# A fused adaLN block on one Trainium2 core: the last V product moved behind the first attention step, another place for the first score tile, and a later reciprocal

## The chip, the core and the metric

The kernel runs on one core of a Trainium2 chip. The core has five engines with queues of their own: PE (TensorE, the matrix products), ACT (ScalarE), DVE (VectorE), POOL (GpSimd) and SP (SyncE, which here issues nearly all DMAs). An engine works its queue strictly in order and waits on semaphores that the others raise. The metric is the device time of one execution in microseconds (us), lower is better. The kernel before takes 1149.5 us, the median of three runs (1148.99 to 1149.98).

## What is computed

One transformer block on x of 2048 tokens by D = 448, all in float32:

```python
x = A_x
mod = (_silu(c) @ w_mod).reshape(c.shape[0], 6, 1, -1)
sa, ca, ga, sb, cb, gb = ...
h = _layernorm(x) * (1 + ca) + sa
x = x + ga * _A_ref(h, A_wqkv, A_wo)          # 16 heads of 28, softmax over 2048 keys
h = _layernorm(x) * (1 + cb) + sb
x = x + gb * _B_ref(h, B_w1, B_b1, B_w2, B_b2)  # layernorm, 448 -> 1792, gelu, 1792 -> 448
```

Softmax is computed with the row maximum taken off, so every query row needs a maximum (or a value close to it) before its exponentials.

## The kernel before, in words

**Tiling.** Tokens come in four blocks of 512 (b, or qt as queries, cch as key chunks). The 16 heads of 28 are padded to 32 and taken in four groups g of four heads j. For precision each operand is split into a float32r part "hi" and a rest "lo", and a product is hi·hi + hi·lo + lo·hi.

**Phase 1** (the loop over `tasks`, line 595 on) makes Q, K and V. A task is (b, kind, g): kind 0 and 1 are Q and K of a head group (`qk_task`, products on line 339), kind 2 is V of 128 tokens (`v_task`, products on line 317, eleven matmuls of 448 columns, then an ACT copy on line 376). Q and K go to DRAM and are read back later. For block b = 3 there are ten tasks, n = 0 to 9: six of Q and K, then V(3,0) to V(3,3). Phase 1 has eight PSUM banks: two "pa" (the accumulators of the tasks, `ps_s`), five "mx" (`ps_mx`) and one "o" (`ps_o`).

**Maxima.** For a unit (g, qt) the maximum is taken over the four key chunks: for each 128 queries i, head j and chunk a one-matmul score (`max_mm`, line 392) goes to an mx tile and DVE reduces it (`max_one`, line 397). A unit has 64 of these. They stand in a list `mxq`, that of unit (0,0) first. `emit_task(n, sixth, n_pairs)` sends a few of them behind each task of phase 1, in place of idle time. Three units, (0,1), (0,2) and (0,3), take their first two chunks as pairs (list `pxq`, `pair_diff`): a product with the difference of the two key chunks, an ACT Relu (line 405), a product with the first chunk, and one DVE instruction that adds and takes the maximum (line 409), so that a pair costs two matmuls, one Relu and one DVE pass. `p1_n` holds what `emit_task` gets: the number of maxima, whether there is a sixth, and how many pairs.

**The shift of a unit.** When the last of a unit's 64 maxima is counted, `max_fin` (line 425) reduces them over the chunks, negated (DVE, line 429). `put`, two steps later (`tick_late`), transposes on DVE (line 436) and sends four small DMAs on SP (line 439), which write the maxima into row 28 of each head's 32 rows of the unit's Q tile (`qst`, tag `b0` or `b1`). The K tiles have ones in that row, so a score comes out with its maximum taken off. The score products of a unit read these rows. Behind the loop of phase 1 stand `finish_max(0, 0)`, which sends what is left of the maxima of unit (0,0), and `tick_late(True)`, which sends a waiting `put` at once (lines 678 and 679).

**Attention** is 16 units u = 4·g + qt of 16 steps (kt, 128 keys each). A step does: scores (line 1045, twelve matmuls in two halves, each into an "s" tile of two banks), three or four maxima of later units in between (`n_maxima`), two ACT exponentials (line 1050) into the tile `pt`, and then the product with V of the step before (`av`, line 1015, into the tile "o"). The tile `pt` rotates over the slots `ptags`. `c0` and `c1` also hold the normalised input of block 3, which V(3,·) reads; `d0` is also the scratch of the Relu of the pairs. In this phase "o" has a pool of its own, `share(3, 2)` gives three mx tiles and two s tiles.

**The end of a unit.** V has a column of ones, so "o" holds the sums of the exponentials too. `unit_end_tasks` lists (offset in steps, function): `t_den` fetches the sums with a DMA, `t_rec` inverts them on DVE (line 774), writes them to DRAM (line 776) and reads them back spread over the rows (line 778), `t_split` multiplies on POOL (line 783), `t_split2` makes hi and lo (DVE line 793, POOL line 794). Units whose output waits in DRAM until the last head group are "staged": units 0 to 10. The others go on to the output product (`t_wo`). The tasks of a unit's end run in steps 1 + offset of the next unit.

**MLP**: products with w1 (line 317 again) and w2 (lines 1102 to 1104), block after block.

Of the kernel before, what the change touches and what calls it, by code (L numbers as in the profile page):

```python
# [18 lines left out]
PSUM = bass.MemoryType.PSUM  # L19
# [9 lines left out]
NB = S // 512  # L29
# [12 lines left out]
def tile_adaln_block(ctx: ExitStack, tc: tile.TileContext, x, wqkv, wo, w1, b1, w2, b2, c, w_mod, out):  # L42
# [322 lines left out]

        return split

    def v_task(b, t):
        p = ps_s()
        ts = slice(t * 128, (t + 1) * 128)  # L370
        hh, hl = hT[b]
        mm_acc(p[:, :D], terms448(
            lambda k: hh(k)[:, ts], lambda k: hl(k)[:, ts], lambda k: wv[0][:, k, :], lambda k: wv[1][:, k, :],
        ))
        emit_task(*p1_n)
        act.copy(v_sb[b][:, t, :, :DH], p[:, :D].rearrange("p (h d) -> p h d", d=DH))


# [221 lines left out]
    for b in range(NB):  # L600
        more = b + 1 < NB
        tasks = []
        for g in range(1 if b else 0, NG):
            tasks += [(b, 0, g), (b, 1, g)]
        if b == 0:
            tasks[1], tasks[2] = tasks[2], tasks[1]
        tasks += [(b, 2, t) for t in range(4)]
        if more:
            stages, later = stages[-4:] if b else stages, ln1_stages(b + 2) if b + 2 < NB else None
            xs_next = []  # L610
            tasks[10:10] = [(b + 1, 0, 0), (b + 1, 1, 0)]
        for n, (tb, kind, g) in enumerate(tasks):
            post = []
            ready, newq = newq, []
            p1_n[0] = P1RATE if b < 1 else P1RATE + 1
            if not more and n == len(tasks) - 1:
                p1_n[0] = 0

            k = n - (5 if b < 2 else 4)
            p1_n[1] = not (more and (0 <= k < NC)) and not (b == 1 and n < 4)  # L620
            p1_n[2] = (3 if n > 4 else 1) if b == 3 else 2 if b == 2 and p1_n[1] else 1
            if kind < 2:
                fn = qk_task(tb, kind, g, 6, firsts[n]) if b == 0 and n < 2 else qk_task(tb, kind, g)
                if g == 0:
                    fn()
                else:
                    post.append(fn)
                if kind == 1 and (g == 0 or (g == 1 and tb < 2)):
                    newq = [(g, qt, cch) for qt in range(tb + 1) for cch in range(tb + 1) if max(qt, cch) == tb]
            else:  # L630
                v_task(tb, g)
            for item in ready:
                queue_max(*item)
            if b == 0 and 2 <= n < 6:
                prep_w(2, n - 2, act.copy, dve)
            if more:
                k = n - (5 if b < 2 else 4)
                if b == 0 and n < 4:
                    for fn in stages[2 * n : 2 * n + 2]:
                        fn(xs_next)  # L640
                if b and n < 4:
                    stages[n](xs_next)
                if 0 <= k < NC:
                    post.append(h_chunk(b + 1, xs_next, k))
                if later and 8 <= n < 12:
                    later[n - 8](None)
            if n == 6:
                v_init(b)
                if b == 0:
                    mod_load(0)  # L650
                    mod_load(1)
            if b == 2 and n == 5:
                sp.dma_start(b1_col, b1.rearrange("(k p) -> p k", p=128))
            if b == 1:
                if n < 2:
                    mod_mm(n)
                    mod_load(2 + n)
                elif n in (2, 3):
                    mod_mm(n)
                    if n == 3:  # L660
                        mod_fin()
            if not more:
                if n == 0:
                    load_q(0)
                    load_q(1)
                if n == 5:
                    load_k(0, 0)
                if n == 6:
                    act.activation(cols[:, 0:1], zero_col, AF.Exp)
                    for ch in range(1, 4):  # L670
                        load_k(0, ch)
            tick_late()
            for fn in post:
                fn()
        if more:
            stages = later
# [3 lines left out]
    ps1_cm.__exit__(None, None, None)  # L680


    o_pool[0] = ctx.enter_context(tc.tile_pool(name="po", bufs=1, space=PSUM))
    shared = []

    def share(n_mx, n_s):
# [3 lines left out]
        psp[:] = [shared[0].__enter__(), n_mx, n_s]  # L690

    share(3, 2)

    phase1[0] = False
    for item in deferred:
# [63 lines left out]
    def unit_end_tasks(u, o_sb):  # L759
        g, qt = divmod(u, NB)  # L760
        st = {}
        staged = g < last_g(qt)
        parts = [g] if g > last_g(qt) else list(range(g + 1))

        def t_den():
            q_ = pool if u == NU - 1 else sp
            den = sbt("den", [128, 16], bufs=2)
            q_.dma_start(den, o_sb[DH:128:32, :].rearrange("j (q r) -> j q r", r=16))
            st["den"] = den

        def t_rec():
            q_ = pool if u == NU - 1 else sp
            rec = st["den"]
            dve.reciprocal(rec, rec)
            drec = dr.tile([4, 512], F32, tag="drec", name=nm("drec"), bufs=2)
            q_.dma_start(drec.rearrange("j (q r) -> (j q) r", r=16), rec)
            rb = sbt("osb", [128, 512], bufs=2)
            q_.dma_start(rb, drec[:, None, :].broadcast_to([4, 32, 512]))
            st["rb"] = rb

        def t_split():
            st["on"] = st["rb"]
            pool.tensor_tensor(out=st["on"], in0=o_sb, in1=st["rb"], op=ALU.mult)  # L783

        def t_split2():
            on = st["on"]
            if u < NU - 1:
                hi = sbt("hi", [128, 512], F32R, bufs=3)
                lo = sbt("lo", [128, 512], F32R, bufs=3)
            else:  # L790
                hi = sb.tile([128, 512], F32R, tag=YTAGS[7], name="o_hi", bufs=1)
                lo = sbt("osb", [128, 512], F32R, bufs=2)
            dve.tensor_copy(hi, on)
            pool.tensor_tensor(out=lo, in0=on, in1=f(hi), op=ALU.subtract)
            st["hi"], st["lo"] = hi, lo
            if staged:
                for part in range(2):
                    sp.dma_start(f(doh[part][g])[:, qt * 512 : (qt + 1) * 512], f((hi, lo)[part]))

        def t_wo(t):  # L800
            def go():
                p = ps_mx()
                ts = slice(t * 128, (t + 1) * 128)
                terms = []
                for g_ in parts:
                    if g_ == g:
                        hi, lo = st["hi"][:, ts], st["lo"][:, ts]
                    else:
                        hi, lo = o_in[(qt, g_)][:, 0, ts], o_in[(qt, g_)][:, 1, ts]
                    w_hi, w_lo = wo_p[0][:, g_, :], wo_p[1][:, g_, :]  # L810
                    terms += [(hi, w_hi), (hi, w_lo), (lo, w_hi)]
                mm_acc(p[:, :D], terms)
                y = sbt("full", [128, 512], bufs=3)[:, :D]
                act.copy(y[:, :D], p[:, :D])  # L814
                pool.tensor_tensor(out=acc[qt][:, t, :], in0=acc[qt][:, t, :], in1=y[:, :D], op=ALU.add)

            return go

        tasks = [(0, t_den), (1, t_rec), (4, t_split), (5, t_split2)]
        if len(parts) > 1 and not staged:  # L820
            tasks.append((0, lambda: load_o(qt)))
        if not staged:
            tasks += [(7 + t, t_wo(t)) for t in range(4)]
        return tasks
# [192 lines left out]
                start=(kt == 0), stop=(kt == NKT - 1),  # L1017
            )

    ptags = ["c0", "c1", "d0"]  # L1020
    done_max = set()
    for u in range(NU):
        g, qt = divmod(u, NB)
        for kt in range(NKT):
# [15 lines left out]
            for hf in range(2):  # L1040
                s2 = ps_s2()
                for term, (kp, qp) in enumerate(((0, 0), (1, 0), (0, 1))):
                    for jj in range(2):
                        rows_ = slice(64 * hf + 32 * jj, 64 * hf + 32 * jj + 32)
                        pe.matmul(s2[:, jj, :], ks[rows_, kp, kc], qs[rows_, qp, :], start=(term == 0), stop=(term == 2))  # L1045
                    if hf == 0 and term < min(n0, n):
                        emit_max(1, 1)
                    if hf == 1 and ((term == 0 and n - n0 > 0) or (term == 2 and n - n0 > 1)):
                        emit_max(1, 0)
                act.activation(pt[:, 2 * hf : 2 * hf + 2, :], s2, AF.Exp, scale=SCALE)  # L1050
            if pend is not None:
                pu, pkt, pp, po = pend
                av(pu, pkt, pp, po)
# [99 lines left out]
```

## Time and profile before

| what | value |
|---|---|
| median of three runs | 1149.5 us |
| the profiled execution's own time | 1151.72 us |
| its span, first to last instruction | 1149.9 us |
| mean granted clock of TensorE | 0.997 |
| PE busy | 1137.5 us (99%) |
| DVE busy | 829.4 us (72%) |
| ACT busy | 682.6 us (59%) |
| POOL busy | 215.9 us (19%) |
| phase 1, first step of attention at | 180.61 us |

A line of the timeline has start, length, engine, line of the code, operation, output <- input, shape and count, and in brackets how long the engine sat idle before it and what ended that. A line of the waits has engine, tile and line <- what it waited for, then total us, number, longest. A line of the windows has the stretch, its length, busy us and count of PE, PEld (weight loads), DVE, ACT and POOL, then the granted clock of TensorE as a share, the DMA share and GB/s. Matmuls overlap, and a busy PE is not PE at its peak.

### The profile page before, as it was taken

The page shows a single profiled execution, that of the slowest core. Times are in us where ns is not written, and L with a number is a line of the kernel's source. Part 1 is how long each engine was busy: PE and PEld are TensorE (multiplying, and loading weights), DVE is VectorE, ACT ScalarE, POOL GpSimd, SP SyncE. Part 2 cuts the span into 40 slices and gives each one's busy share as a digit, 9 for nine tenths or more (in the row PEclk, how much of TensorE's full clock was granted, in tenths as well). Part 3 has the DMA queues.
Part 4 walks back from the last instruction along what each step waited for, and adds up shares of the span by engine and source line. Part 5 has one row for each costly group of instructions (what it writes and reads, how often), then busy time and mean ns, then how long its engine had stood idle before and what let it go on. Part 6 is the DMA issues. An engine that isn't in the chain of part 4 may idle for free.

```text
span 1149.9 us, 20811 instructions
## 1 busy us (share of the span) xinstructions
PE 1137.5 (99%) x8380; PEld 680.7 (59%) x8380; DVE 829.4 (72%) x1487; ACT 682.6 (59%) x839; POOL 215.9 (19%) x232
## 2 busy tenths in 40 slices
PE   8999999999999999999999999999999999999998
PEld 6767774444444444444444445545458888888887
DVE  6868787999888899989999876585448853444322
ACT  4666756777777887877777777675862321111110
POOL 2534431210000000000000011207214503223000
PEclk9999998999999999999999999999999999999999
DMA  9642354121132211321111221020323100000000
GB/s 301 205 147 111 101 184 129 38 66 57 35 98 73 57 38 38 91 65 56 53 57 30 84 84 53 33 84 2 118 62 95 43 33 1 1 32 1 32 1 32
DMA packets 51377, 81.08 MB, mean 71 GB/s; under 512 B 12728, under 2 KB 21772, under 8 KB 51280
## 3 DMA queue, kind: packets, MB, share of 16 engines
q1 hardware_dynamic: 50656, 79.01, 22.1%
q8 instruction: 66, 1.08, 0.4%
q10 hardware_dynamic: 288, 0.46, 0.1%
q0 software_dynamic: 336, 0.28, 0.1%
q14 instruction: 31, 0.25, 0.1%
HBM read 53.11 MB, written 26.35 MB: 69 GB/s over the span
## 4 chain that ended last, share of the span: by engine, by line
PE 95%; DMA 1%; DVE 1%; ACT 1%; issue 1%; SPq 0%; POOL 0%; DVEq 0%; POOLq 0%; ACTq 0%
PE s L1045 27%; PE o L1015 21%; PE mx L317 16%; PE pa L339 7%; PE mx L392 7%; PE s L1103 4%; PE s L1102 4%; PE s L1104 4%; PE pa L317 3%; PE o L240 1%; PE pa L276 1%; DMA drec<-den 1%; DMA osb<-drec 1%; ACT slot_c L1050 1%; PE mx L240 0%
## 5 line engine op out<-in xcount | busy, mean ns | idle before, releaser
L397 DVE TENSOR_REDUCE mxp<-mx 128x1 f32<-128x512 f32 x919 | 579.9, 684 | 106.5 <-PE mx L392 101.5
L1045 PE MATMUL s<-slot_b,slot_a 32*128 32x512 f32 x3072 | 385.5, 424 | 1.9 <-ACT full L814 0.7
L1050 ACT ACTIVATE slot_c<-s 128x1024 f32<-128x1024 f32 x342 | 331.6, 1022 | 86.3 <-PE s L1045 84.7
L1045 PEld LDWEIGHTS s<-slot_b,slot_a 32*128 32x128 f32 x3072 | 215.9, 184 | 255.2 <-ACT slot_c L1050 151.5
L392 PE MATMUL mx<-kh,qh 32*128 32x512 f32 x899 | 290.9, 471 | 1.4 <-DVE mxp L397 1.1
L1050 ACT ACTIVATE slot_d<-s 128x1024 f32<-128x1024 f32 x170 | 164.8, 1022 | 44.6 <-PE s L1045 44.5
L1015 PE MATMUL o<-slot_c,v 128*32 128x512 f32 x1368 | 184.4, 609 | 0.4 <-ACT osb L984 0.4
L1086 ACT ACTIVATE full<-mx,b_col 128x512 f32<-128x512 f32 x56 | 38.5, 688 | 191.9 <-PE mx L317 179.8
L1089 DVE CAST hi<-full 128x512 fp32r<-128x512 f32 x56 | 25.2, 450 | 135.3 <-ACT full L1086 135.3
L392 PEld LDWEIGHTS mx<-kh,qh 32*128 32x128 f32 x899 | 116.6, 182 | 9.6 <-DVE mxp L397 6.7
L783 POOL TENSOR_TENSOR osb<-osb,osb 128x512 f32<-128x512 f32 x16 | 20.9, 1307 | 484.3 <-DMA osb<-drec 412.3
L1015 PE MATMUL o<-slot_d,v 128*32 128x512 f32 x680 | 90.6, 605 | 0.0
L1015 PEld LDWEIGHTS o<-slot_c,v 128*32 128x32 f32 x1368 | 27.1, 108 | 57.5 <-issue 54.0
L317 PE MATMUL mx<-y,slot_a 128*128 128x512 f32 x160 | 60.6, 395 | 0.0
L405 ACT ACTIVATE slot_d<-mx 128x512 f32<-128x512 f32 x48 | 27.0, 596 | 40.1 <-PE mx L392 40.0
L1090 DVE TENSOR_TENSOR lo<-full,hi 128x512 fp32r<-128x512 f32 x56 | 44.1, 788 | 5.2
L317 PE MATMUL mx<-y,slot_c 128*128 128x512 f32 x152 | 47.5, 396 | 0.1
L1104 PE MATMUL s<-slot_v,lo 128*128 128x448 f32 x128 | 46.7, 365 | 0.0
L1102 PE MATMUL s<-slot_v,hi 128*128 128x448 f32 x128 | 46.6, 364 | 0.0
L317 PE MATMUL mx<-y,slot_v 128*128 128x512 f32 x112 | 39.2, 396 | 0.0
L317 PE MATMUL mx<-y,slot_b 128*128 128x512 f32 x112 | 39.0, 397 | 0.0
L339 PE MATMUL pa<-slot_c,slot_a 128*128 128x512 f32 x136 | 36.9, 405 | 0.0
(223 smaller groups left out, 1386.9 us busy)
## 6 DMA issues: line engine op xcount, KB each, us to landing
d<-lo SPq DMA_DIRECT2D x32, 256.0 KB
slot_b<-d SPq DMA_DIRECT2D x32, 256.0 KB
slot_a<-d SPq DMA_DIRECT2D x32, 256.0 KB
d<-hi SPq DMA_DIRECT2D x20, 256.0 KB
osb<-drec SPq DMA_DIRECT2D x15, 256.0 KB
out_dram<-xn SPq DMA_DIRECT2D x16, 224.0 KB
slot_v<-in_w_mod_dram SPq DMA_DIRECT2D x4, 784.0 KB
raw<-in_B_w_dram SPq DMA_DIRECT2D x14, 224.0 KB
```

What stands on the lines that cost most here:

```text
L317: pe.matmul(p, a, b, start=(i == 0), stop=(i == len(terms) - 1))
L339: pe.matmul(p, *ts[i], start=(i == 0), stop=(i == len(ts) - 1))
L392: pe.matmul(m, qh_sb[(g, qt)][js, i * 128 : (i + 1) * 128], k[js, :], start=True, stop=True)
L397: dve.tensor_reduce(out=mxp[(g, qt)][:, i, j, cch : cch + 1], in_=m, op=ALU.max, axis=AX.X)
L1015: pe.matmul(o[32 * j : 32 * j + 32, :], v_sb[kt // 4][:, kt % 4, 4 * g + j, :], p[:, j, :], start=(kt == 0), stop=(kt == NKT - 1),)
L1045: pe.matmul(s2[:, jj, :], ks[rows_, kp, kc], qs[rows_, qp, :], start=(term == 0), stop=(term == 2))
L1050: act.activation(pt[:, 2 * hf : 2 * hf + 2, :], s2, AF.Exp, scale=SCALE)
L1086: act.activation(gf, p, AF.Gelu_apprx_tanh, bias=b1_col[:, i : i + 1])
L1090: dve.tensor_tensor(out=glo, in0=gf, in1=f(ghi), op=ALU.subtract)
L1102: pe.matmul(pp, ghi[:, ts], w_hi, start=(m == 0), stop=False)
L1103: pe.matmul(pp, ghi[:, ts], w_lo, start=False, stop=False)
L1104: pe.matmul(pp, glo[:, ts], w_hi, start=False, stop=(m == NFT - 1))
```

## The change

Four edits.

- In phase 1 the tasks of block 3 are nine, not ten: V(3,3) is taken out of the list. Its products are issued in step 0 of attention, behind the step's scores and ahead of the product with V (there is none in step 0), into an mx tile, and three maxima are sent behind it.
- What phase 1 sends beside block 3's tasks: three pairs a task from n = 3 on and not from n = 5 on; in the last task (now n = 8, V(3,2)) two maxima, and its product goes to an mx tile and not to a pa tile.
- The pool of "o" is opened behind that of the s and mx tiles and on the other side of PSUM, so the first s tile lies on the two banks that were pa; `ptags` starts with `d0`.
- Staged units run `t_rec`, `t_split` and `t_split2` in offsets 4, 8 and 9, not 1, 4 and 5.

```diff
-    def v_task(b, t):
-        p = ps_s()
+    def v_task(b, t, p):
...
-        emit_task(*p1_n)
+        if phase1[0]:
+            emit_task(*p1_n)
         act.copy(v_sb[b][:, t, :, :DH], p[:, :D].rearrange("p (h d) -> p h d", d=DH))
...
-        tasks += [(b, 2, t) for t in range(4)]
+
+        tasks += [(b, 2, t) for t in range(4 if more else 3)]
...
             if not more and n == len(tasks) - 1:
-                p1_n[0] = 0
+                p1_n[0] = 2
 
             k = n - (5 if b < 2 else 4)
             p1_n[1] = not (more and (0 <= k < NC)) and not (b == 1 and n < 4)
-            p1_n[2] = (3 if n > 4 else 1) if b == 3 else 2 if b == 2 and p1_n[1] else 1
+            p1_n[2] = (3 if n > 2 else 1) if b == 3 else 2 if b == 2 and p1_n[1] else 1
...
-                v_task(tb, g)
+                v_task(tb, g, ps_mx() if p1_n[0] == 2 else ps_s())
...
-    o_pool[0] = ctx.enter_context(tc.tile_pool(name="po", bufs=1, space=PSUM))
     shared = []
...
     share(3, 2)
+    o_pool[0] = ctx.enter_context(tc.tile_pool(name="po", bufs=1, space=PSUM, side="right"))
...
-        tasks = [(0, t_den), (1, t_rec), (4, t_split), (5, t_split2)]
+
+        times = (0, 4, 8, 9) if staged else (0, 1, 4, 5)
+        tasks = list(zip(times, (t_den, t_rec, t_split, t_split2)))
...
-    ptags = ["c0", "c1", "d0"]
+    ptags = ["d0", "c0", "c1"]
...
                 act.activation(pt[:, 2 * hf : 2 * hf + 2, :], s2, AF.Exp, scale=SCALE)
+            if step == 0:
+                v_task(NB - 1, 3, ps_mx())
+                emit_max(3)
             if pend is not None:
```

## The prediction

> **What bounds the kernel now.** I read the page first (engines, chain), then the waits of PE and DVE, then the timeline of each engine where the change acts, then windows for the clock.
>
> ```profile
> PE 1137.5 (99%) x8380; PEld 680.7 (59%) x8380; DVE 829.4 (72%) x1487; ACT 682.6 (59%) x839; POOL 215.9 (19%) x232
> PE 95%; DMA 1%; DVE 1%; ACT 1%; issue 1%; SPq 0%; POOL 0%; DVEq 0%; POOLq 0%; ACTq 0%
> DVE den L774 <- DMA den<-osb: 8.6, 3, 4.4
> DVE hi L793 <- POOL osb L783: 2.9, 3, 1.7
> POOL osb L783 <- DMA osb<-drec: 412.3, 13, 37.4
> ```
>
> PE is the bound: 99% busy, 95% of the chain that ended last. A change pays only where it shortens PE's stream or a hole in it. Two places are touched. One is the seam between phase 1 and attention:
>
> ```profile
> 174.27 2.50 PE L317 MATMUL pa<-slot_e,slot_c 128*128 128x448 f32 x11
> 176.70 0.50 PE L392 MATMUL mx<-raw,qh 32*128 32x512 f32 x3
> 177.45 2.53 PE L317 MATMUL pa<-slot_e,slot_c 128*128 128x448 f32 x11
> 180.61 0.50 PE L1045 MATMUL s<-slot_b,slot_a 32*128 32x512 f32 x2 [0.62 <-ACT v L376]
> 182.74 0.50 PE L1045 MATMUL s<-slot_b,slot_a 32*128 32x512 f32 x2 [0.28 <-ACT slot_c L1050]
> 185.23 1.94 PE L1015 MATMUL o<-slot_c,v 128*32 128x512 f32 x8
> 189.43 1.51 PE L1015 MATMUL o<-slot_c,v 128*32 128x512 f32 x8
> 194.82 1.07 PE L1015 MATMUL o<-slot_c,v 128*32 128x512 f32 x8
> 180.00:183.00 3.00, 1.97 (x19) 1.15 (x21) 1.78 (x3) 1.87 (x3) 0.00 (x0) 1.00 1.05 393
> 183.50:184.00 0.50, 0.50 (x6) 0.35 (x5) 0.50 (x2) 0.33 (x2) 0.00 (x0) 0.55 0.93 185
> 186.00:189.00 3.00, 3.00 (x24) 1.47 (x16) 1.04 (x2) 0.58 (x2) 2.99 (x4) 0.50 0.15 41
> 190.00:190.50 0.50, 0.50 (x8) 0.00 (x0) 0.49 (x1) 0.50 (x1) 0.00 (x0) 0.62 0.30 86
> ```
>
> V(3,2) runs from 174.27, six products for maxima from 176.70, V(3,3) from 177.45; the first scores wait 0.62 us for its copy, step 1 waits 0.28 us for an exponential. In 180 to 183 PE is busy 1.97 of 3.00 us, and the granted clock then halves from about 183.55 to 190.4, some 6.8 us (0.55 and 0.62 are the slices in which it turns). So the first product with V comes 4.62 us after the first score, and the next three steps take 194.82 − 185.23 = 9.59 us. The other place is the reciprocal:
>
> ```profile
> 349.11 1.07 PE L1015 MATMUL o<-slot_d,v 128*32 128x512 f32 x8
> 351.33 1.06 PE L1015 MATMUL o<-slot_c,v 128*32 128x512 f32 x8
> 356.12 1.06 PE L1015 MATMUL o<-slot_c,v 128*32 128x512 f32 x8
> 351.15 0.58 SPq L768 DMA_DIRECT2D den<-osb  x1
> 353.05 0.26 DVE L774 RECIPROCAL den<-den 128x16 f32<-128x16 f32 x1 [2.63 <-DMA den<-osb]
> 346.37 1.06 PE L1015 MATMUL o<-slot_c,v 128*32 128x512 f32 x8
> 511.95 1.06 PE L1015 MATMUL o<-slot_c,v 128*32 128x512 f32 x8
> 515.68 1.06 PE L1015 MATMUL o<-slot_d,v 128*32 128x512 f32 x8
> 512.62 0.25 DVE L774 RECIPROCAL den<-den 128x16 f32<-128x16 f32 x1 [1.57 <-DMA den<-osb]
> ```
>
> Undisturbed steps take 2.74 and 2.22 us in turn (346.37, 349.11, 351.33). At 353.05 DVE stands still for the sums of unit 3; no maxima are reduced, PE finds no free mx tile, and the step takes 4.79 us. Unit 7 does the same at 512.62 with 3.73 us.
>
> **The change, part by part.**
>
> *The pairs come earlier, and that leaves maxima over.* This is the step that decides, and it stands in no line of the diff by itself. The 16 pairs of unit (0,3) are there from n = 1, and so are 16 singles of unit (0,0), its last key chunk, which head the list. A task with one pair sends four singles, a task with three sends none. Before: four singles in each of n = 1 to 4, so all 16 are out with n = 4. After: four in n = 1 and 2, none in n = 3 to 6, two in n = 7 (beside the last two pairs), two in n = 8. That is 12. The other four come from `finish_max(0, 0)`, behind V(3,2). In the built program's order six products of qh0 with kh3 stand between V(3,2) and the first score, where before there is only V(3,3). Only then is unit (0,0) complete; its reduction, transposition and four DMAs follow, and the first score reads what these write. Before, this was long past:
>
> ```profile
> 167.47 0.22 DVE L429 TENSOR_REDUCE m<-mxp 128x16 fp32r<-128x64 f32 x1
> 170.61 2.36 SPq L439 DMA_DIRECT2D slot_b<-full  x4
> 174.43 1.55 ACT L405 ACTIVATE slot_d<-mx 128x512 f32<-128x512 f32 x3
> 181.22 4.28 DVE L397 TENSOR_REDUCE mxp<-mx 128x1 f32<-128x512 f32 x7 [1.43 <-PE mx L392]
> 180.02 0.53 ACT L376 COPY v<-pa 128x448 f32<-128x448 f32 x1 [0.79 <-PE pa L317]
> 170.37 0.21 DVE L436 STREAM_TRANSPOSE full<-m 128x32 f32<-128x32 f32 x1
> ```
>
> Now the chain, with these durations, in before's time. V(3,2) started at 174.27 in pa; in mx it takes the tile of n = 7's first Relu, which is through at 174.43 + 0.52 + 0.1, so it runs 175.05 to 177.5 (its own 2.50 us). The six maxima follow. DVE starts its first reduction 0.61 us after the product (181.22 against 180.61): 178.1; six at 0.61 (4.28/7) end at 181.8. Reduction and transposition, 0.2 each: 182.2. SP issues four DMAs in 2.36 us, the last starting at 184.0; a small DMA lands 1.9 us after its issue starts (351.15 to 353.05): the first score at T = 185.9. PE has been idle since about 179.4, 6.5 us. Bounds of T: 185.3 (landing in 1.3 us) and 186.5.
>
> *V(3,3) behind step 0's scores.* The stretch from first score to first product with V was 4.62 us. V adds 2.53 us at full clock and 5.06 at half; it covers 0.41 us of holes (of the 1.03 us without PE in 180 to 183, less the 0.62). The third of the extra maxima takes V's mx tile and waits for its copy (0.53) and a reduction: 0.8 us, with 0 and 1.8 (three reductions in series) as ends. After a 6.5 us hole I expect half clock, as the smaller hole brought it. How long it lasts after T depends on a phase I don't know; I take 5 us, with the row's 6.8 as the long end, so V takes 3.8. First product with V: T + 4.62 + 3.8 − 0.41 + 0.8 = T + 8.8 = 194.7; ends T + 6.7 and T + 11.1. Three more steps at full clock are 7.4 us: 202.1 against 194.82, **+7.3 us** (185.3 + 6.7 + 7.4 gives +4.6; 186.5 + 11.1 + 7.4 gives +10.2).
>
> [...]
>
> *First s tile on the pa banks, d0 first.* The 0.62 us wait for V(3,3)'s copy goes, but the wait for the DMAs stands at the same place and covers it: nothing. `d0` is read last by the pairs' DVE pass, in n = 7: no wait. Step 1 writes `c0` only after V(3,3), which PE has done by then.
>
> *SP behind the moved DMAs.* The four now stand behind the K loads and ahead of three loads of maxima operands and of 16 wo loads.
>
> ```profile
> 177.59 1.39 SPq L420 DMA_DIRECT2D kh<-d  x2
> 179.98 12.46 SPq L726 DMA_DIRECT2D raw<-in_A_wo_dram  x16
> 200.94 0.38 DVE L733 CAST slot_e<-full 128x448 fp32r<-128x448 f32 x1
> ```
>
> These move back by some 7.6 us, but the DVE work on wo is in step 6 and moves back by 7.3 with the steps: nothing; without that cover, a DVE hole of up to 0.3.
>
> *Three maxima more in step 0.* The number in all stays, so three fewer come later, at the end of the list: −0.3 us (a step of four costs 2.74, one of three 2.22).
>
> *The later reciprocal.* It is asked for 3 steps (7.4 us) later, against holes of 2.63 and 1.57 us: both go. PE gains 4.79 − 2.74 and 3.73 − 2.74, 3.0 us. The 4.4 us hole in the wait's row is the last unit's, which isn't staged: it stays. Of the 2.9 us that DVE waits for POOL, 1.7 is one wait, I take it for the last unit's too; the other two, 0.6 each, cost PE between nothing (the holes above cost it 0.58 less than they are long) and 1.2: I take 0.4. Sum −3.4. Ends: −4.2 (all of 2.63 and 1.57) and −2.0, if the transfers, now between the K loads of steps 3 and 7, come late to step 9 and DVE waits anew. What is queued behind these waits is the maxima, and PE behind them.
>
> **Sum.** +7.3 − 0.3 − 3.4 = +3.6 us: span 1149.9 to 1153.5, the profiled execution 1151.72 to 1155.3. The median of the runs is 2.2 below that execution, so 1149.5 + 3.6 = **1153.1 us**.
>
> **Rivals.**
> - *The shift is in time (other side).* If the four DMAs landed by the time PE is through with the six maxima, 178.3, PE would have no hole, the clock would stay: first product with V at 178.3 + 6.7, three steps to 192.4, −2.4, with −3.4 and −0.3 that is −6.1: 1143.4. It speaks for it that before they had landed long ahead; against it that six reductions alone take 3.7 us behind the last product. It decides from T below 180.5. 0.09.
> - *The seam costs less.* The clock comes back at once and the extra maxima hide: at T + 6.7 it is +5.2, sum +1.5: 1151.0. For it: the phase is open. Against: 6.8 us in the row. 0.21.
> - *The reciprocal's gain isn't there.* New waits of the split and cast at steps 9 and 10 take the place of the old ones. For it: POOL waits for this transfer 13 times. Against: POOL has nothing else to do then, and DVE waited for it only 2.9 us in all. At zero gain and +7.3 − 0.3: 1156.5. 0.13.
>
> **How the numbers follow.** My own case has 0.57 and spans 1151.9 to 1155.2. A measurement tells 0.2%, 2.3 us, from no change: 1147.2 to 1151.8. Faster is the first rival, 0.09; the same is the second, 0.21; slower the rest, 0.70. For 8 in 10 I leave out the first rival and the outermost of the third: 1149.0 to 1156.5, which takes in the ends +0.1 (4.6 − 4.2 − 0.3) and, short of +7.9, most of the upper one.
>
> **What would show it.** Six reductions (line 397) behind V(3,2), then lines 429, 436 and four of 439 at about 182; a first score whose idle time of about 6.5 us ends on a DMA; half clock for 3 to 7 us behind it; V(3,3) between the scores of steps 0 and 1, in mx; no reciprocal of a staged unit with a wait ahead of it; steps of 2.74 at units 4 and 8. I am wrong if the first score starts below 182, if the clock stays full, or if new DVE waits show at line 793.

## The result, and the profile after

The changed kernel takes 1157.3 us (median of six runs, 1156.3 to 1159.2) against 1149.7 us for the kernel before on the same chip (six runs, 1148.6 to 1154.0): a ratio of 1.0057, interval 1.0042 to 1.0072, some 6.6 us slower. The profiled execution of the changed kernel took 1156.97 us, with a span of 1155.2 us and a mean granted clock of 0.995 (before: 1151.72, 1149.9, 0.997).

From the page of the changed kernel, busy time by engine and the chain by engine:

```profile
PE 1136.9 (98%) x8380; PEld 683.1 (59%) x8380; DVE 829.9 (72%) x1487; ACT 682.6 (59%) x839; POOL 215.9 (19%) x232
PE 95%; DVE 1%; ACT 1%; DMA 1%; issue 1%; SPq 0%; DVEq 0%; ACTq 0%
```

PE does the same work (1136.9 us, before 1137.5) in a span that is 5.3 us longer, so what was lost on balance is time in which PE stood idle. The waits of PE and DVE (engine, tile and line, what it waited for; us in total, number, longest) say which, and which went:

```profile
PE s L1048 <- DMA slot_b<-full: 6.6, 1, 6.6
PE mx L317 <- ACT slot_d L405: 0.7, 1, 0.7
DVE den L775 <- DMA den<-osb: 4.4, 1, 4.4
DVE hi L794 <- POOL osb L784: 2.4, 2, 1.7
```

One hole of 6.6 us is new: the first score waits for a DMA that writes its operand. Two of the three DVE waits for the sums of units are gone; the last unit's 4.4 us stays.

The seam in the timeline of the changed kernel, PE first, then what goes on meanwhile on DVE, SP's queue and ACT:

```profile
168.67 2.52 PE L317 MATMUL pa<-slot_e,slot_c 128*128 128x448 f32 x11
175.69 2.50 PE L317 MATMUL mx<-slot_e,slot_c 128*128 128x448 f32 x11 [0.72 <-ACT slot_d L405]
178.12 0.50 PE L392 MATMUL mx<-kh,qh 32*128 32x512 f32 x4
178.81 1.08 PE L392 MATMUL mx<-kh,qh 32*128 32x512 f32 x2 [0.19 <-ACT v L376]
186.53 0.79 PE L1048 MATMUL s<-slot_b,slot_a 32*128 32x512 f32 x2 [6.64 <-DMA slot_b<-full]
188.91 3.83 PE L317 MATMUL mx<-slot_e,slot_c 128*128 128x448 f32 x11
195.81 1.06 PE L1018 MATMUL o<-slot_d,v 128*32 128x512 f32 x8
198.54 1.06 PE L1018 MATMUL o<-slot_c,v 128*32 128x512 f32 x8
203.50 1.07 PE L1018 MATMUL o<-slot_d,v 128*32 128x512 f32 x8
...
178.65 3.68 DVE L397 TENSOR_REDUCE mxp<-mx 128x1 f32<-128x512 f32 x6 [1.31 <-PE mx L392]
182.37 0.22 DVE L429 TENSOR_REDUCE m<-mxp 128x16 fp32r<-128x64 f32 x1
182.68 0.21 DVE L436 STREAM_TRANSPOSE full<-m 128x32 f32<-128x32 f32 x1
182.92 2.33 SPq L439 DMA_DIRECT2D slot_b<-full  x4
```

The first row is V(3,0), from which I count below, since phase 1 ends up to some 2 us earlier or later from one profile to the next (V(3,0) starts at 168.03 to 170.22 us, and at 172.17 in the one kernel whose edit made phase 1 longer). V(3,2) and the six products of maxima are over at 179.9. Then DVE reduces six maxima, four of them the ones left over, closes the unit and transposes; SP issues four DMAs; the first score starts at 186.53. V(3,3) stands between the scores of steps 0 and 1 and takes 3.83 us instead of 2.53. From V(3,0) to the fourth product with V it is 203.50 − 168.67 = 34.83 us; before it was 194.82 − 168.03 = 26.79, with V(3,0) at

```profile
168.03 2.52 PE L317 MATMUL pa<-slot_e,slot_c 128*128 128x448 f32 x11
```

I call this stretch the seam: +8.04 us.

Windows of the same trace (stretch, its length, busy time and instructions of PE, PEld, DVE, ACT and POOL, the granted clock, the share and rate of the DMA engines):

```profile
181.00:181.50 0.50, 0.00 (x0) 0.00 (x0) 0.50 (x2) 0.00 (x0) 0.00 (x0) 1.00 0.04 16
181.50:182.00 0.50, 0.00 (x0) 0.00 (x0) 0.50 (x2) 0.00 (x0) 0.00 (x0) 0.61 0.00 0
186.00:191.50 5.50, 4.97 (x23) 3.90 (x24) 2.48 (x4) 1.94 (x2) 0.00 (x0) 0.50 0.71 207
191.50:192.00 0.50, 0.50 (x4) 0.44 (x3) 0.00 (x0) 0.00 (x0) 0.12 (x1) 0.65 0.12 36
```

The clock halves at about 181.6, 1.7 us after PE's last matmul, and comes back at about 191.85: 10.24 us in all, 5.3 us of it behind the first score. (The edges come from the slices in which the mean lies between 0.5 and 1: a mean of 0.61 over 0.5 us is 0.39 us at half clock.)

The places of the old reciprocal holes, from the third product with V of a unit to the fourth, in units 4 and 8:

```profile
359.84 1.06 PE L1018 MATMUL o<-slot_d,v 128*32 128x512 f32 x8
362.58 1.06 PE L1018 MATMUL o<-slot_c,v 128*32 128x512 f32 x8
...
518.40 1.06 PE L1018 MATMUL o<-slot_c,v 128*32 128x512 f32 x8
521.14 1.06 PE L1018 MATMUL o<-slot_c,v 128*32 128x512 f32 x8
```

The steps that took 4.79 and 3.73 us both take 2.74.

### The profile page after: what moved, and what is told of

It reads as the page before. It is cut to its first block, busy times and chain, and to the rows that moved or that the text cites. A ratio compares the mean times of both kernels' runs of the same rounds, so it can differ in the third digit from the quotient of the medians.

```text
span 1155.2 us, 20815 instructions
## 1 busy us (share of the span) xinstructions
PE 1136.9 (98%) x8380; PEld 683.1 (59%) x8380; DVE 829.9 (72%) x1487; ACT 682.6 (59%) x839; POOL 215.9 (19%) x232
## 4 chain that ended last, share of the span: by engine, by line
PE 95%; DVE 1%; ACT 1%; DMA 1%; issue 1%; SPq 0%; DVEq 0%; ACTq 0%
PE s L1048 28%; PE o L1018 22%; PE mx L317 16%; PE pa L339 7%; PE mx L392 6%; PE s L1109 4%; PE s L1110 4%; PE s L1108 4%; PE pa L317 3%; DMA slot_c<-in_w_mod_dram 1%; PE o L240 1%; PE mx L240 1%; DVE mxp L397 0%; PE o L547 0%; DMA acc<-in_A_x_dram 0%
## 5 line engine op out<-in xcount | busy, mean ns | idle before, releaser
L1018 PE MATMUL o<-slot_c,v 128*32 128x512 f32 x1360 | 181.2, 605 | 0.0
```

What stands on the lines that cost most here:

```text
L1018: pe.matmul(o[32 * j : 32 * j + 32, :], v_sb[kt // 4][:, kt % 4, 4 * g + j, :], p[:, j, :], start=(kt == 0), stop=(kt == NKT - 1),)
```

## The experiments

The theory at the start: the three pairs from n = 3 leave four maxima over, these put the first score behind a chain of reductions and DMAs, and the half clock that the hole brings makes the moved V product dear; the later reciprocal gives back a little over 3 us. The rival: moving the V product loses by itself. Each kernel is given with the edit against the one it starts from.

**The pairs as late as before, in the changed kernel** (e1_pairs_late).

```diff
-            p1_n[2] = (3 if n > 2 else 1) if b == 3 else 2 if b == 2 and p1_n[1] else 1
+            p1_n[2] = (3 if n > 4 else 1) if b == 3 else 2 if b == 2 and p1_n[1] else 1
```

> The kernel after, with three pairs a task from n = 5 on again (as before), so that no maxima of unit (0,0) are left over behind phase 1; all else stays changed. Theory (the shift of unit (0,0) is late): the DMA wait of the first score, 6.6 us, is gone; the first score waits only for the copy of V(3,2), which now stands behind three Relus, and starts about 180.3 to 181; V(3,3) and three maxima still lie between the scores, so the first product with V comes 7.4 to 9 us behind; with the later reciprocals 1146 to 1149 us, some 9 us under the kernel after. Rival (moving V(3,3) between the scores is itself what costs): 1155 us or more, whatever the wait.

1152.67 us, ratio 1.0013 (1.0004 to 1.0022, eleven runs): 5.1 us better than the change (0.0044 of 1150), yet not faster than before, as had been expected. Its timeline:

```profile
181.96 0.50 PE L1048 MATMUL s<-slot_b,slot_a 32*128 32x512 f32 x2 [1.56 <-DVE mxp L409]
184.03 4.48 PE L317 MATMUL mx<-slot_e,slot_c 128*128 128x448 f32 x11
192.61 1.94 PE L1018 MATMUL o<-slot_d,v 128*32 128x512 f32 x8
```

The wait for the DMAs is gone. In its place the first score waits 1.56 us for DVE's last pair pass, although that reads the o tile, on other banks than the first score's. It starts 12.67 us behind V(3,0) (169.29 in this trace); before it was 180.61 − 168.03 = 12.58, with V(3,3) already done by then. So taking V(3,3) from ahead of the first score did not bring the score forward, and V then costs its full length behind it, 4.48 us at half clock. The seam is 32.51 us, 5.7 longer than before. The time lies between the theory (1146 to 1149) and the rival (1155 or more): the theory missed, and the rival gains.

**The earlier pairs alone, in the kernel before** (e2_pairs_early_alone): the line above the other way round.

```diff
-            p1_n[2] = (3 if n > 4 else 1) if b == 3 else 2 if b == 2 and p1_n[1] else 1
+            p1_n[2] = (3 if n > 2 else 1) if b == 3 else 2 if b == 2 and p1_n[1] else 1
```

> The kernel before with one edit: three pairs a task from n = 3 on. V(3,3) stays in phase 1. One maximum of unit (0,0) is left over behind V(3,3). Theory: its reduction, line 429, 436 and the four DMAs hold the first score until about 185.5 (180.6 before), a wait of about 5 us for a DMA, half clock behind it: 1153.5 to 1155. Rival (the order of the maxima costs nothing): 1149.7 within 1.

1156.8 us, ratio 1.0051 (1.0037 to 1.0064): 5.9 us, somewhat over what was expected. Timeline:

```profile
186.31 0.79 PE L1045 MATMUL s<-slot_b,slot_a 32*128 32x512 f32 x2 [4.93 <-DMA slot_b<-full]
191.61 1.94 PE L1015 MATMUL o<-slot_c,v 128*32 128x512 f32 x8
```

V(3,3) now fills part of the hole, but the first score comes as late as in the change (186.31 − 169.10 = 17.21 us behind V(3,0); in the change 17.86). One number in one line costs 5 to 6 us in either kernel.

**The later reciprocal alone, in the kernel before** (e3_reciprocal_alone).

```diff
-        tasks = [(0, t_den), (1, t_rec), (4, t_split), (5, t_split2)]
+        times = (0, 4, 8, 9) if staged else (0, 1, 4, 5)
+        tasks = list(zip(times, (t_den, t_rec, t_split, t_split2)))
```

> The kernel before with one edit: staged units run the reciprocal, the split and the cast in offsets 4, 8 and 9. Theory: the long steps of units 4 and 8 (4.79 and 3.73 us) go back to 2.74, the wait of line 774 keeps only its 4.4 us of the last unit; 3.4 us gained, 1146.3 (1145.3 to 1147.7). Rival (new waits at the later place eat it): 1149.7 within 1, with waits of line 793 on POOL in several units.

1147.5 us, ratio 0.9972 (0.9961 to 0.9983): −3.2 us, as expected. It is faster than both kernels.

**The clock kept up in the hole of the changed kernel** (e6_keep_warm). 24 products with the identity, which nobody reads, ahead of the first score.

```diff
     tick_late(True)
+    busy = ps_s()
+    for _ in range(24):
+        pe.matmul(busy[:, :128], ident, ident, start=True, stop=True)
     ps1_cm.__exit__(None, None, None)
```

> The kernel after, with 24 matmuls of the identity (128 columns, as at the kernel's start, into a pa tile that nobody reads) behind the left-over maxima, to keep PE busy in the hole. Theory (hole and half clock add): the first score starts where it did, 186.5, but the clock stays at or near 1.0, V(3,3) takes 2.5 and not 3.8 us, the first product with V comes about 7.4 us behind the first score and not 9.3: about 2 us less than the kernel after, 1155.3. Rival (the half clock is hidden behind DVE and ACT): same as the kernel after, 1157.3 within 0.7.

```profile
186.12 0.50 PE L1051 MATMUL s<-slot_b,slot_a 32*128 32x512 f32 x2 [1.08 <-DMA slot_b<-full]
188.08 2.53 PE L317 MATMUL mx<-slot_e,slot_c 128*128 128x448 f32 x11
193.68 1.07 PE L1021 MATMUL o<-slot_d,v 128*32 128x512 f32 x8
```

The clock stays at 1.0, V takes 2.53 us, the first product with V comes 7.56 us behind the first score instead of 9.28, and the seam is 33.12 us, 1.7 shorter than in the change. The runs don't show a gain: 1157.71 us, ratio 1.0064 (1.0043 to 1.0085, four runs from 1155.9 to 1162.2). Three of the four ran at a mean granted clock of 0.999 or more and took 1155.9 to 1158.1 us, about what the change takes at 0.992 to 0.995 (1156.3 to 1159.2). So what the half clock costs the change isn't shown by the times; whether the 24 products cost as much as they save was not separated.

**V(3,3) back ahead of the first score, in the hole** (e7_v_in_the_hole). The first step's three extra maxima go too.

```diff
     tick_late(True)
+    p1_n[0] = 0
+    v_task(NB - 1, 3, ps_s())
     ps1_cm.__exit__(None, None, None)
...
-            if step == 0:
-                v_task(NB - 1, 3, ps_mx())
-                emit_max(3)
```

> The kernel after, with V(3,3) issued behind the left-over maxima and ahead of step 0 (into a pa tile), not between the scores of steps 0 and 1; the three extra maxima go too. Theory (the shift's DMAs set the first score): the first score starts where it did, about 17.9 us behind V(3,0), V(3,3) costs nothing in the hole, the first product with V comes 5.3 us behind the first score (9.3 in the kernel after): about 2.5 us less than the kernel after. Rival (V between the scores is hidden behind the exponentials): same as the kernel after within 0.7 us.

1154.52 us, ratio 1.0039 (1.0025 to 1.0053): 2.8 us less than the change by the medians, 2.1 by the ratios, with about 2.5 expected.

```profile
179.90 2.49 PE L317 MATMUL pa<-slot_e,slot_c 128*128 128x448 f32 x11
186.62 0.79 PE L1050 MATMUL s<-slot_b,slot_a 32*128 32x512 f32 x2 [4.22 <-DMA slot_b<-full]
191.91 1.94 PE L1020 MATMUL o<-slot_d,v 128*32 128x512 f32 x8
```

The first score starts where it did (17.88 us behind V(3,0)); the first product with V comes 5.29 us behind it instead of 9.28. So in the change V(3,3) and the three maxima behind it lie on the path, beside a hole in which V would have been free. Of these 3.99 us the three steps behind take back 1.45 (9.14 us against 7.69), since the half clock here lasts until 195.23, 8.6 us behind the first score. The seam is 2.5 us shorter.

**The moved V without the leftover, another way** (e8_v_move_no_leftover). In the changed kernel one maximum more per task for n = 1 to 4, and three pairs from n = 4.

```diff
-            p1_n[0] = P1RATE if b < 1 else P1RATE + 1
+            p1_n[0] = P1RATE if b < 1 else P1RATE + 2 if not more and 1 <= n <= 4 else P1RATE + 1
...
-            p1_n[2] = (3 if n > 2 else 1) if b == 3 else 2 if b == 2 and p1_n[1] else 1
+            p1_n[2] = (3 if n > 3 else 1) if b == 3 else 2 if b == 2 and p1_n[1] else 1
```

> The kernel after, with six maxima instead of five beside tasks n = 1 to 4 of block 3 and three pairs from n = 4 on: all 16 maxima of unit (0,0) are out with n = 4, and one pair instead of three stands beside the last task. Theory (moving V(3,3) loses by itself, because the first score still waits for all readers of phase 1's tiles, and V then lies on the path): the first score about 12.5 us behind V(3,0) as before the change, the first product with V 7.4 to 10 us behind it (4.6 before the change); against the kernel before +3 to +5 from the seam and -3.3 from the reciprocals: same to 0.2 per cent slower. Rival (only the left-over maxima and the late pairs cost): 4 to 5 us faster than the kernel before.

1154.95 us, ratio 1.0044 (1.003 to 1.0057), worse than expected.

```profile
183.57 0.50 PE L1048 MATMUL s<-slot_b,slot_a 32*128 32x512 f32 x2 [1.24 <-ACT v L376]
185.51 4.05 PE L317 MATMUL mx<-slot_e,slot_c 128*128 128x448 f32 x11
```

No DMA wait is left, but V(3,0) starts at 172.17 us, where the other profiles have 168.0 to 170.2: the added maxima made phase 1 itself some 2 to 4 us longer. So the time is no test of the seam; by the ratios of this run and the first experiment the four maxima cost some 3.6 us when moved ahead in this way, and 5.1 left over. The seam itself, counted from V(3,0), is 200.31 − 172.17 = 28.14 us, only 1.4 longer than before. With one pair instead of three beside the last task the first score comes 11.40 us behind V(3,0), and the half clock lasts 3.41 us. So what the moved V costs depends on the work beside V(3,2) and on the clock: the seam grows by 1.4 us here and by 5.7 in the first experiment.

**The places alone** (e11_banks_alone). In the kernel with the later reciprocal, the o pool on the right side, so that the first score tile lies on the pa banks, and V(3,3) in an mx tile, still ahead of the first score.

```diff
-        p = ps_s()
+        p = ps_mx() if (b, t) == (NB - 1, 3) else ps_s()
...
-    o_pool[0] = ctx.enter_context(tc.tile_pool(name="po", bufs=1, space=PSUM))
     shared = []
...
     share(3, 2)
+    o_pool[0] = ctx.enter_context(tc.tile_pool(name="po", bufs=1, space=PSUM, side="right"))
```

> The kernel before with the later reciprocals, the pool of o on the other side (first s tile on the two pa banks) and V(3,3) in an mx tile. Theory (the first tile of the new pool waits for all readers of the old pool): the first score still sits idle about 0.6 us for the ACT copy of V(3,3), though that tile lies in another bank. Rival (the wait is by bank): no wait, the first score follows V(3,3) at once.

One time, 1149.69 us, and one timeline:

```profile
178.81 2.49 PE L317 MATMUL mx<-slot_e,slot_c 128*128 128x448 f32 x11 [0.35 <-ACT slot_d L405]
181.93 0.50 PE L1046 MATMUL s<-slot_b,slot_a 32*128 32x512 f32 x2 [0.62 <-ACT v L376]
```

No phase 1 tile on the first score's banks is in use any more, and yet the score waits the same 0.62 us for the copy of V(3,3), which reads an mx tile. The pair pass on the o tile in the first experiment fits with this. In both cases (0.62 and 1.56 us) the first tile of the new pools waits for the last reader of a tile of the old pool that lies on other banks. (Which banks a tile has follows here from the order in which the kernel opens its pools; the trace names tiles, not banks.)

**The moved V alone** (e12_v_move_alone). The first experiment's kernel with the old reciprocal times, so neither leftover nor gain.

```diff
-        times = (0, 4, 8, 9) if staged else (0, 1, 4, 5)
+        times = (0, 1, 4, 5)
```

> The changed kernel with three pairs from n = 5 and the reciprocal's old times, so that no maxima are left over and the reciprocal's gain is out: only the moved V product, its mx tile, the swapped pools, the first maxima of step 0 and d0 first. Theory: moving the V product loses by itself, since the first score still waits for the last reader of phase 1's tiles and V then lies on the path at half clock: e1_pairs_late's +1.5 us with the reciprocal's 3.2 us taken back, +4.7 us, ratio 1.003 to 1.005; seam longer by 5 to 6 us. Rival: the reciprocal's gain is small beside the moved V product (its waits come at other places there), and the move costs little: ratio below 1.0025.

1154.96 us, ratio 1.0039 (1.0027 to 1.0051, twelve runs): 4.5 us, as the theory had it by now.

```profile
181.23 0.79 PE L1048 MATMUL s<-slot_b,slot_a 32*128 32x512 f32 x2 [1.56 <-DVE mxp L409]
183.59 4.40 PE L317 MATMUL mx<-slot_e,slot_c 128*128 128x448 f32 x11
191.07 1.86 PE L1018 MATMUL o<-slot_d,v 128*32 128x512 f32 x8
```

Again the first score comes 12.67 us behind V(3,0) (168.56), V takes 4.40 us, and the seam is 200.17 − 168.56 = 31.61 us, +4.8. One part of the rival's reason is seen all the same: with the old reciprocal times DVE waits only 0.27 us for the sums of unit 7 here, against 1.57 before, and the step takes 2.74 us; only unit 4's long step (4.36 us) is left.

**Later reciprocal, with and without filler** (e10_reciprocal_and_filler, then both once more beside each other). The filler is three products with the identity behind V(3,3) and four behind the scores of step 0, again read by nobody.

```diff
     tick_late(True)
+    busy = ps_s()
+    for _ in range(3):
+        pe.matmul(busy[:, :128], ident, ident, start=True, stop=True)
...
+            if step == 0:
+                idle = ps_mx()
+                for _ in range(4):
+                    pe.matmul(idle[:, :128], ident, ident, start=True, stop=True)
```

> The kernel before with the later reciprocals and filler: three matmuls of the identity behind V(3,3), four behind step 0's scores, which nobody reads. Theory (half clock in the seam of the kernel before costs some 2 to 3 us): the clock stays at 1.0, the three steps behind the first product with V take 7.5 us and not 9.6: 2 us less than the later reciprocals alone, 4.5 to 5.5 us faster than before. Rival (DVE and ACT set the pace there, as where filler was tried in the kernel after without a clear gain): the same as the later reciprocals alone, 3.2 us faster.

> e3_reciprocal_alone once more, beside the kernel with filler products on the same chip. Theory: ratio 0.996 to 0.9985 against the kernel before.

> e10_reciprocal_and_filler once more (seven products with the identity that nobody reads, beside the later reciprocal). Theory A: the clock kept full in the seam is worth what the profile showed, 1 to 2 us: a ratio 0.001 to 0.0015 below that of e13_reciprocal_again. Theory B: the runs show none of it (the filler delays what it stands ahead of, or the clock falls elsewhere): the two ratios within 0.0005 of each other, or the filler's higher.

With filler: 1148.67 us, ratio 0.9981 (0.9971 to 0.9992), then 1148.72 us, 0.9975 (0.9963 to 0.9988). Without: 1147.16 us, 0.9971 (0.9957 to 0.9985). The filler is not seen to gain anything, as theory B has it. It costs time itself: of the last two kernels, on one chip, the runs at a mean granted clock of 0.999 or more have a median of 1148.3 us with filler (9 of 12) and 1146.9 without (7 of 10). The seam accounts for 0.5 us of this (194.92 − 170.22 = 24.70 us in the last profile with filler; 24.20 without, below); where the rest lies was not found. And the filler did not keep the clock up everywhere: that profile has it at half from about 23.5 to 27 us (means of 0.97 from 0 to 25 us and of 0.96 from 25 to 50), far ahead of the seam. Why there is little to gain shows in two profiles of the same kernel, the later reciprocal alone. First execution, 1149.38 us:

```profile
180.00:184.00 4.00, 2.95 (x25) 1.72 (x25) 2.60 (x7) 2.13 (x4) 0.00 (x0) 1.00 1.05 397
184.00:188.00 4.00, 4.00 (x23) 1.38 (x23) 2.61 (x5) 2.77 (x3) 0.52 (x1) 0.57 0.51 142
```

Second execution, 1146.93 us:

```profile
180.00:184.00 4.00, 3.00 (x23) 1.73 (x21) 2.57 (x7) 2.10 (x5) 0.00 (x0) 1.00 1.05 402
184.00:188.00 4.00, 3.95 (x38) 1.85 (x38) 3.37 (x6) 2.99 (x4) 0.96 (x1) 1.00 0.61 163
```

The same holes (2.95 and 3.00 of 4 us busy), and the clock halves in one execution and not in the other. The seam is 195.91 − 169.19 = 26.72 us in the first and 193.55 − 169.35 = 24.20 in the second: 2.5 us, as much as the two times lie apart (2.45). So these small holes go with the half clock in some executions only (5 of the 17 runs of this kernel have a mean granted clock below 0.999), and there is little left for a filler to save.

**The kernel before, profiled again** (e15_before_again), no edit.

> The kernel before, unchanged, profiled once more. The same kernel with the later reciprocal showed the seam at half clock in one profiled execution (1149.38 us) and at full clock in another (1146.93 us), 2.45 us apart. Theory: the profiled execution of before (1151.72 us, 2.2 us above the median of its runs) is one with the half clock, and most of its runs have none: this one then shows full clock in 183 to 192 us, steps of 2.74, 2.16 and 2.80 us behind the first product with V, and a time of 1148.5 to 1150 us. Rival: the kernel before halves its clock there in nearly every execution, and the 2.2 us come from elsewhere: half clock again at 183 to 192 us, whatever the time.

```profile
181.03 0.49 PE L1045 MATMUL s<-slot_b,slot_a 32*128 32x512 f32 x2 [0.62 <-ACT v L376]
186.00:188.00 2.00, 2.00 (x12) 0.48 (x8) 0.00 (x0) 0.78 (x1) 1.09 (x2) 0.50 0.19 54
```

1151.25 us, and again at half clock; the run beside it took 1149.38 us at a mean granted clock of 1.0, against 0.997. The rival's picture came out for this execution, but not its reason: of the 59 runs of before beside the other experiments, 32 ran at 0.999 or more. Both profiled executions of before have the half clock, and both lie about 2 us above what most runs take.

## Why the prediction was right, and where it was wrong

The direction held (0.70 on slower). The forecast was +3.6 us, and 6.6 came. On the 1149.5 us that the forecast started from, the ratio gives 1156.1 us (1154.3 to 1157.8), just inside the range that ended at 1156.5 and above the 1155.2 of its own case; the median itself, 1157.3, lies 0.8 us above the range. In 1150 us the parts that the runs separate are, in order, before → moved V alone → with the later reciprocal → with the earlier pairs: ratios 1, 1.0039, 1.0013, 1.0057, that is **+4.5, −3.0, +5.1 us**, together +6.6. Each part has an interval of some 1.4 to 2 us to either side, the runs were made on different chips (each against before on its own), and another order would divide the sum otherwise.

- *The pairs leave maxima over, and the chain starts the first score late.* Right in mechanism and size. T, the first score, was forecast at 185.9 in before's time; it is 186.53 in a trace that runs 0.64 us later by then, so 185.89. Six reductions, lines 429 and 436, four DMAs at 182.92 and a hole of 6.64 us (6.5 forecast) are all there. The last of the DMAs starts at 184.73, 1.80 us ahead of the score (1.9); the landing in 1.3 us of T's lower bound was an estimate that no run shows. Two experiments, with and without the leftover, price it at 5.9 and 5.1 us.
- *V(3,3) behind step 0's scores.* V takes 3.83 us (3.8; the 5.06 us for a V wholly at half clock were twice 2.53, and late pairs, where it ran so, took 4.48), the half clock lasts 5.3 us behind T (5), the first product with V comes 9.28 us behind T (8.8). The three steps behind it take 203.50 − 195.81 = 7.69 us (7.4), since the steps run at 2.73, 2.16 and 2.80. With 0.5 and 0.3 us more, the seam is +8.04 instead of +7.3: the term that was mis-sized, by 0.7 us, inside its own ends.
- *The 0.62 us wait for V(3,3)'s copy goes.* Wrong in its reason. In two cases, the places alone (0.62 us) and the late pairs (1.56 us), the first score waited for a reader of a phase 1 tile on other banks than its own. Here the DMA wait covers it, so the price of nothing stands. But the same error makes the first rival, "the shift is in time", wrong by its own condition: with the DMAs landed in time, it had the first product with V at 178.3 + 6.7 and 1143.4 us; the kernel with the late pairs has its DMAs landed in time and takes 1152.67 us, because the first score still waits until 181.96 and V then runs at half clock (in its profile, the slowest of its runs). The forecast counted 5.3 us for the late T and 4.2 for V behind it, less 2.2 for steps at full clock; it did not see that V's place loses by itself, 4.5 us by the runs, also where T is not late.
- *The later reciprocal, −3.4.* Right for the kernel before: −3.2 us alone, −3.3 when repeated. In the profiles, from the fourth product with V to the first of unit 12, before takes 666.85 − 194.82 = 472.0 us, the later reciprocal alone 468.7, the change 672.12 − 203.50 = 468.6. Part of the gain by the ratios may be the clock: runs at 0.999 or more, compared on the same chip, give −2.2 and −2.5 us. With the V product moved the same stretch takes 670.94 − 200.17 = 470.8 us, and with the later reciprocal beside it 670.58 − 201.80 = 468.8: 2.0 us there, since unit 8's hole was gone already, and not the 3.0 of the ratios. In the change both steps went to 2.74 us, the last unit's 4.4 us stayed, DVE's waits for POOL fell by 0.5 only, and no new wait came. The rival without the gain is out.
- *Three maxima more in step 0, −0.3; the moved DMAs of SP, nothing.* Neither was separated. The sum of the terms leaves 8.04 + 0.64 − 5.25 = 3.4 us of gain behind the seam in the profiles, for the reciprocal's −3.4 and this −0.3 together.
- *From the profiled execution to the median.* This step failed most. The sum gave 1155.3 us for the profiled execution; it took 1156.97, of which 0.64 us had passed by the start of V(3,0) and 0.7 is the seam. Then I took off 2.2 us, since before's profiled execution lay that far above its median. The change's profiled execution lies at its median (1156.97 against 1157.3). The table holds the hole ahead of the first score against this difference:

| kernel | hole, us | half clock in the profile, us | profiled | median | runs at 0.999 or more |
|---|---|---|---|---|---|
| before | 0.62 | 6.8 | 1151.72 | 1149.7 | 32 of 59 |
| later reciprocal alone | 0.62 | 6.8 | 1149.38 | 1147.5 | 5 of 7 |
| the same, again | 0.62 | none | 1146.93 | 1147.2 | 7 of 10 |
| V moved, more maxima per task | 1.24 | 3.41 | 1153.94 | 1155.0 | none of 5 |
| moved V alone | 1.56 | 10.24 | 1155.46 | 1155.0 | none of 12 |
| late pairs in the change | 1.56 | 13.65 | 1156.17 | 1152.7 | 2 of 11 |
| V in the hole | 4.22 | 10.24 | 1154.41 | 1154.5 | none of 4 |
| earlier pairs alone | 4.93 | 10.24 | 1156.43 | 1156.8 | none of 4 |
| the change | 6.64 | 10.24 | 1156.97 | 1157.3 | none of 6 |

The last column counts runs by the mean granted clock of the whole execution, which is on record for each (for before, the runs beside the experiments). A stretch of 6.83 us at half clock takes this mean to 0.997, one of 10.24 us to 0.995 or 0.996 (the profiles in the table). The 32 runs of before at 0.999 or more took 1148.2 to 1150.9 us (median 1149.5), the other 27, at 0.994 to 0.998, took 1150.2 to 1155.4 (median 1152.1), and its profiled execution is one of the latter. All six runs of the change lie at 0.992 to 0.995. So the 2.2 us were the distance between an execution of before at half clock and its usual one at full clock, and the change has no such usual one. Where no run is at full clock, profile and median agree within half a microsecond, the moved V alone with its small hole included (the kernel with more maxima per task, whose profile has the highest clock of its five runs, lies 1.0 us below its median). The mean does not say where the clock fell; that it fell in the seam is shown for the profiled executions only.

The traces show when the clock fell and came back, and not by what rule. In the change it fell 1.7 us into the hole, with PE busy for 1.61 of the 3.00 us from 178 to 181; in before it fell at about 183.55 with no hole over 0.62 us, PE busy for 1.97 of the 3.00 us from 180 to 183. It came back 5.3 us behind T in the change, and at about 190.38 in before, 9.8 us behind the first score. The forecast's 5 us was the author's estimate, with the row's 6.8 as its long end; the phase on which the prediction makes it depend is shown by no run.

## What to carry to other kernels

Look for what an edit does to the order of a list that it does not name: here one threshold for pairs left four maxima over, and these stood ahead of the first score with a whole chain of reductions and DMAs behind them. Moving work from ahead of a wait to behind it gains only if the wait ends earlier by it; ask what else the wait ends on, and whether the place that the work leaves becomes an empty hole. And convert a sum from a profiled execution to a median only after asking in which clock that execution and the other runs ran: executions of the same kernel differ here by 2 us and more with it (1149.38 and 1146.93 us for the later reciprocal alone), and the difference does not carry over to a kernel of which every run is at half clock.

## What was not expected of the hardware

- The stretches at half clock in the profiles of these seams come out near one, two, three or four times 3.41 us: 3.41 (V moved, more maxima per task), 6.83 (before, the later reciprocal, the places alone), 6.83 and 3.41 with full clock between (the moved V alone), 10.24 (the change, the earlier pairs alone, V in the hole), 13.65 (late pairs). No run shows why.
- The clock stayed at half with PE busy in the profile. In before PE is busy for all of the 3.41 us from 183.55 to 186.96, at a granted clock of 0.50, and the clock comes back only at about 190.38. Late pairs in the change, windows:

```profile
184.00:187.00 3.00, 3.00 (x9) 2.67 (x9) 1.05 (x2) 0.97 (x2) 0.00 (x0) 0.50 0.69 190
187.00:190.00 3.00, 2.92 (x10) 1.38 (x8) 0.74 (x2) 0.53 (x1) 2.63 (x4) 0.50 0.09 23
190.00:193.00 3.00, 2.99 (x17) 1.75 (x21) 2.94 (x5) 1.30 (x2) 0.45 (x2) 0.50 0.38 113
193.00:196.50 3.50, 3.50 (x24) 1.47 (x16) 1.15 (x2) 1.08 (x2) 0.00 (x0) 0.50 0.04 14
```

PE is shown as busy for 12.4 of 12.5 us, and the clock stays at half throughout. What brings the clock back, these runs don't tell.
